# Element-wise steps of a fused linear-attention and GCU kernel offered to GpSimd, with a new fixed schedule

## The chip, the cores and the metric

The kernel runs on one core of a Trainium2 chip. The metric is the device time of one launch in microseconds (us), as the median over runs; lower is better.

## What is computed

Eight batches of eight heads, 576 tokens, head size 64, go through a linear attention, and the result through a two-matrix layer with a cosine gate:

```python
theta = np.pi / 2.0 * pos / S
def phi(x, c, s):                       # c, s: cos and sin of theta, one value per token
    r = np.maximum(x, 0.0)
    return np.concatenate([r * c, r * s], axis=-1)
q_p, k_p = phi(q, cos_w, sin_w), phi(k, cos_w, sin_w)
kv  = np.einsum('bhsf,bhsd->bhfd', k_p, v)
z   = np.sum(k_p, axis=2)
num = np.einsum('bhsf,bhfd->bhsd', q_p, kv)
den = np.einsum('bhsf,bhf->bhs', q_p, z)[..., None] + 1e-06
x   = (num / den)                       # then (4608, 512)
h   = x @ w_in                          # 512 -> 2048
g   = h * np.cos(h)
out = g @ w_out                         # 2048 -> 512
```

## The kernel before

**Stages.** The 4608 tokens are worked in nine chunks of 512. Chunks 0 to 7 hold 512 tokens of one batch each; the 64 tokens left over in each batch make chunk 8, the last one, which therefore has no attention of its own. For a batch, q, k and v are loaded in float32 (`load`), and for each of five token groups `t` and each of cosine and sine (`g`) one step `prep` makes a *feature*: a tile of 128 partitions by 512 elements, `max(x, 0)` times one value per partition, read as float32 and written as float16 into the tile `KQ`. That is 20 features a batch (10 of q, 10 of k; odd or even batches leave some of q out, so some have 18). `cast_v` copies v to float16. `kv` and `num` are the small attention matmuls, the result is normalised on VectorE (lines 449 to 453) and transposed. `layer1(c)` multiplies by `w_in` and applies the gate `h * cos(h)`: ScalarE takes the sine of `h + pi/2` into `ch` (line 503), then a multiplication makes `gT` (line 505). `layer2` multiplies by `w_out`.

**Seven products for eight.** `layer2` and a part of `layer1` do a 2 by 2 block product with seven block products and some additions (Strassen's way). In `layer1_fast` a group of four column blocks takes 28 matmuls of 256 columns in place of 16 of 512; its price is three copies on ScalarE (line 674) and three additions on VectorE (line 678) into the float32 SBUF tile `Z`. Two of its gates then read SBUF alone: one of 128x512 (from `Y`) and one of 128x1024 (line 695, from `U` and `Z` together). The rest of the gates read one operand from PSUM; no step of GpSimd in this kernel reads PSUM. `FAST1` says how many of the four groups of each chunk are done so.

**The order.** Nothing is scheduled while building. Every step is put on a list with `Plan.add`; `STARTS` holds a number for each step, and the steps are issued in the order of these numbers. `ENGS` holds a letter for each step: P TensorE, D VectorE, A ScalarE, G GpSimd, S the SP queue. A step made by `either` has code for several engines and the letter chooses. On each engine the instructions run in that order; between engines, semaphores hold the data dependences. Steps marked `port=True` (features, casts of v, sums and differences with both operands in SBUF, SBUF gates) get one thing more: where one of them on VectorE (D) follows one on GpSimd (G) in the list, or the other way round, a semaphore makes the later one wait for the earlier one (line 1091). So VectorE and GpSimd never work on such steps at the same time. I call a run of marked GpSimd steps between two marked VectorE steps a *turn*. VectorE steps that are not marked (gates from PSUM, additions from PSUM, normalisations) may run during a turn.

**GpSimd before.** It casts v in batches 2 to 7 (three steps a batch, line 360), issues the weight loads, and issues the stores of the output (lines 731, 744, 748) and two pairs of accumulating copies (line 818). It computes no feature and no gate. There are seven turns. The features of batches 2 to 7 stand on ScalarE (88) and VectorE (26), those of batches 0 and 1 on both as well (17 and 21).

Of the kernel before, what the change touches and what calls it, by code (L numbers as in the profile page):

```python
# [11 lines left out]
ALU = mybir.AluOpType  # L12
# [6 lines left out]
    53, 0, 0, 74, 139, 204, 269, 334, 399, 464, 543, 1050, 1190, 1280, 1100, 1370, 2014, 2134, 2044,  # L19
    843, 841, 923, 1134, 801, 717, 865, 1541, 885, 779, 969, 1524, 759, 717, 819, 1298, 1014, 1050,  # L20
    1174, 1245, 1112, 1287, 1092, 1203, 1050, 1380, 1236, 1422, 1430, 1329, 1393, 1354, 1473, 1504,
    1498, 1467, 1447, 1487, 1561, 1636, 1635, 1708, 1733, 1860, 1745, 1995, 2030, 1720, 1696, 1745,
    1831, 1921, 1956, 2018, 1983, 2080, 2030, 2208, 2270, 1896, 1909, 1965, 2098, 2133, 2121, 2220,
    2290, 2231, 2330, 2400, 2456, 2555, 2625, 2369, 2468, 2538, 2543, 2642, 2712, 2718, 2817, 2887,
    2630, 2730, 2800, 2805, 2904, 2974, 2979, 3078, 3148, 2892, 2991, 3061, 3066, 3166, 3384, 3241,
    3340, 3445, 3154, 3253, 3323, 3489, 3626, 3707, 3576, 3738, 3936, 3402, 3576, 3646, 1812, 1852,
    1917, 1792, 1982, 2047, 3802, 3922, 3832, 1772, 1752, 2284, 2349, 2662, 2893, 3590, 3514, 3506,
    3676, 4262, 3390, 3548, 3788, 3768, 3452, 3852, 3850, 4033, 4091, 3810, 4123, 4252, 4358, 3894,
    3962, 4297, 4355, 4039, 4296, 4512, 4639, 3997, 4024, 4467, 4524, 4160, 4086, 4211, 4185, 4186,
    4304, 4259, 4237, 4222, 4330, 4343, 4405, 4479, 4584, 4596, 4711, 4846, 4891, 4559, 4571, 4596,  # L30
    4806, 4841, 4834, 4869, 4933, 5301, 5611, 4781, 4794, 4818, 5054, 5089, 5189, 5164, 5630, 5756,
    5791, 3688, 3912, 3861, 4539, 4079, 4589, 4609, 5139, 4881, 5279, 5323, 5777, 7362, 7472, 5583,
    6356, 5953, 6207, 9668, 7417, 5213, 5313, 5569, 5077, 5189, 5340, 5866, 6065, 6146, 5779, 6015,
    6085, 5496, 5903, 6006, 6300, 6399, 6478, 6213, 6337, 6417, 6125, 6225, 6295, 6598, 6757, 6881,
    6511, 6645, 6715, 6710, 6869, 6942, 7007, 7155, 7230, 6797, 6981, 7064, 7107, 7206, 7423, 7416,
    7540, 7692, 7194, 7368, 7484, 5038, 5165, 8219, 9256, 4387, 4322, 4517, 4687, 4452, 4849, 5487,
    5425, 5443, 5401, 5549, 5527, 5363, 5485, 5735, 5661, 6134, 6024, 6244, 6449, 6387, 6585, 5838,
    5880, 5940, 5953, 5841, 6081, 6275, 5964, 6470, 5922, 6449, 6761, 6698, 6685, 6776, 6984, 7256,
    7094, 6972, 7125, 7393, 7428, 7281, 7293, 7318, 7528, 7640, 7503, 7515, 7587, 7725, 7760, 6552,
    7814, 7941, 6885, 7306, 7590, 7551, 7638, 7753, 8497, 8390, 8650, 9257, 8131, 8935, 9060, 9330,  # L40
    9418, 9836, 9616, 9789, 10202, 11508, 11870, 9963, 10050, 10149, 11705, 10219, 7872, 7994, 8097,
    7958, 8056, 8158, 8044, 8230, 8333, 8218, 8342, 8436, 8304, 8454, 8653, 8478, 8576, 8793, 8564,
    8662, 8732, 8762, 8898, 8968, 9047, 9145, 9370, 8849, 8948, 9029, 9244, 9431, 9536, 9505, 9603,
    9733, 9133, 9481, 9958, 9703, 9801, 10019, 9877, 9975, 10141, 10187, 10285, 10467, 5631, 5795,
    6886, 6966, 6269, 6334, 6807, 6523, 7478, 6919, 7306, 7031, 7093, 7545, 6695, 6666, 7082, 7192,
    7302, 7748, 7810, 7934, 7810, 7872, 7954, 8168, 8055, 8250, 8392, 8106, 8539, 8280, 8394, 8846,
    8712, 8836, 9240, 8750, 8737, 8854, 9050, 9034, 9022, 9090, 9383, 9219, 9232, 9431, 9554, 9604,
    9591, 9628, 9751, 10162, 10137, 10263, 10949, 7003, 9195, 9897, 10080, 10589, 10764, 11104,
    10273, 10448, 10757, 10919, 11248, 11498, 12495, 11378, 11478, 11857, 11776, 12496, 12595,
    11950, 12149, 12773, 12731, 12967, 13314, 13496, 14205, 13055, 13272, 13371, 13441, 14370,  # L50
    10368, 10401, 10434, 11071, 10360, 10416, 10404, 10528, 10607, 10703, 10597, 10657, 10640,
    10707, 10876, 11010, 10832, 10888, 11103, 11218, 11192, 11247, 11437, 10684, 10869, 10949,
    11007, 11359, 11559, 11578, 11757, 11954, 11093, 11645, 11893, 11335, 11595, 11664, 11725,
    12093, 12320, 11707, 11807, 11863, 11919, 11907, 12015, 12037, 12093, 12211, 12381, 12106,
    12161, 12259, 12323, 12421, 12609, 12409, 12533, 12712, 12645, 12881, 12951, 12237, 12831,
    13253, 7605, 7670, 8474, 8971, 8664, 7735, 9307, 8998, 8504, 8611, 9195, 9531, 9794, 9369, 8774,
    9653, 9388, 9498, 9608, 10535, 10770, 11043, 9851, 9715, 10079, 10466, 10025, 10664, 10335,
    9913, 10417, 10807, 10981, 11174, 11179, 11235, 11332, 11538, 11466, 11565, 11620, 11743, 11751,
    11763, 11788, 11911, 12081, 12093, 12154, 12277, 13139, 13375, 13789, 13471, 13602, 13707,
    13775, 13906, 14086, 15133, 14079, 14167, 14359, 14695, 14782, 14899, 14496, 15068, 15308,  # L60
    15377, 15892, 16236, 17499, 17279, 15464, 15551, 15713, 15783, 15838, 12876, 13106, 13073,
    13531, 12880, 12936, 12924, 13012, 13533, 13728, 13228, 13284, 13359, 13421, 13427, 13564,
    13558, 13625, 13757, 13903, 13862, 13955, 14025, 13142, 13843, 14147, 13689, 14067, 14313,
    14297, 14471, 14587, 13993, 14571, 14814, 14254, 14309, 14452, 14526, 14949, 15072, 14409,
    14521, 14608, 14663, 14651, 14753, 14894, 15011, 15173, 15369, 14938, 15061, 15247, 15291,
    15663, 15733, 14981, 15501, 15588, 15639, 15763, 15873, 15204, 15551, 15649, 9876, 9941, 11452,
    11336, 10854, 10789, 11533, 11409, 11695, 11471, 12297, 12031, 10919, 12359, 11969, 11297,
    11760, 11595, 11448, 12818, 12583, 13172, 12645, 12670, 12730, 13110, 13489, 13614, 12471,
    12769, 12875, 13048, 12707, 13970, 12986, 12834, 14196, 13402, 13415, 14208, 14331, 14396,
    14384, 14421, 15154, 14595, 14583, 14648, 14771, 14869, 14882, 14906, 15029, 15155, 15180,  # L70
    15483, 16450, 15947, 16122, 16592, 16153, 16284, 16383, 16569, 16700, 17266, 17943, 16787,
    16918, 17154, 17334, 17224, 17402, 17818, 18067, 17315, 17601, 17837, 18296, 18513, 18625,
    19136, 19316, 18122, 18209, 18401, 18471, 18526, 19226, 19046, 15794, 16297, 15840, 16391,
    15849, 15904, 15980, 16061, 16215, 16330, 16110, 16165, 16240, 16296, 16371, 16531, 16415,
    16470, 16631, 16767, 16657, 16717, 16881, 16483, 16581, 16706, 16023, 16953, 17047, 17005,
    17104, 17718, 17116, 17378, 17468, 16875, 17003, 17246, 17302, 17478, 17548, 17203, 17428,
    17545, 17601, 17502, 17779, 17775, 17840, 17919, 18057, 17992, 18117, 18213, 17905, 18239,
    18358, 17688, 18189, 18485, 18383, 18675, 18745, 18035, 18351, 18588, 12441, 12506, 13549,
    13739, 13096, 13014, 13583, 13686, 13645, 14117, 14837, 13471, 13893, 14005, 14999, 14409,
    14035, 14260, 14145, 15787, 15725, 15954, 15383, 15321, 15465, 14775, 14713, 14896, 15813,  # L80
    15601, 15960, 15111, 15259, 16741, 16458, 16471, 16942, 17398, 17092, 17104, 17150, 17273,
    17302, 17290, 17363, 17523, 17489, 17589, 17613, 17736, 18819, 18946, 19442, 19228, 19414,
    19513, 18811, 18942, 19041, 20535, 19687, 19774, 19873, 19943, 19998, 20439, 20915, 21027,
    20171, 20302, 20632, 21177, 21438, 21537, 21733, 21643, 21002, 21089, 21463, 21588, 21533,
    22885, 22975, 18419, 18452, 18649, 19060, 18469, 18575, 18600, 18682, 18761, 19198, 18768,
    18871, 18899, 18954, 19184, 19259, 19054, 19320, 19399, 19556, 19501, 19650, 19836, 19098,
    19277, 19381, 19327, 19700, 19775, 19973, 20071, 20291, 19600, 19923, 20125, 19544, 19600,
    19930, 20003, 20121, 20352, 19886, 19973, 20128, 20183, 20072, 20413, 20259, 20474, 20682,
    20788, 20526, 20582, 20710, 20570, 20768, 21007, 20742, 21077, 21190, 20829, 20927, 21129,
# [92 lines left out]
def kernel(  # L182
# [9 lines left out]
    nc = tc.nc  # L192
    B, H, S, D = q.shape
# [89 lines left out]
    pl = Plan()  # L283
# [839 lines left out]
```

## Time and profile before

| what | value |
|---|---|
| median of 3 runs | 282.94 us (282.44 to 284.58) |
| the profiled execution | 285.63 us, its span 283.9 us |
| granted clock of TensorE, mean | 0.984 |
| busy: TensorE matmul | 96% of the span |
| busy: VectorE, ScalarE, GpSimd | 85%, 72%, 20% |
| HBM read and written | 36.75 and 11.80 MB |

A profiled execution is one run; its span is the time from its first to its last instruction, and the run's own time is 1.7 us longer. The "busy" share of an engine counts only time in instructions. Matmuls overlap, so the duration of a single matmul is longer than the spacing from one to the next; what a matmul costs is read from the spacing.

### The profile page before, as it was taken

The numbers are of one execution on the slowest core, as the hardware profiler recorded it, in microseconds if no ns is written. First come the engines' busy times: TensorE is split into PE (matmuls) and PEld (weight loads), VectorE is DVE, ScalarE is ACT, GpSimd is POOL, SyncE is SP. The second block draws the span as 40 slices with busy tenths as digits, with TensorE's granted clock in tenths as the row PEclk, the third lists the DMA queues.
The fourth block names the chain that finished last, engine by engine and source line by source line (L and its number), as shares of the span: only waits on it lengthen the run. The fifth ranks groups of instructions, "written<-read, shape, count | busy, mean of one in ns | idle before, by whom it ended". The sixth has DMA issues, their size and how long they took to land.

```text
span 283.9 us, 6672 instructions
## 1 busy us (share of the span) xinstructions
PE 272.2 (96%) x2635; PEld 210.9 (74%) x2635; DVE 241.3 (85%) x447; ACT 205.3 (72%) x357; POOL 57.7 (20%) x87
## 2 busy tenths in 40 slices
PE   7699999999999999999999999999999999999993
PEld 2557857669976677877867777787768888876882
DVE  1666798999999999997989999999998979987742
ACT  2646699589989979998988959995736687676030
POOL 1322020021500310140150102415101343230410
PEclk9599999999999999999999999999999999999998
DMA  6999989969999999999998999989323949693515
GB/s 190 316 189 241 256 270 217 354 192 242 238 341 240 262 226 191 209 339 258 291 229 199 216 324 200 220 189 163 102 57 95 180 120 110 172 134 67 113 74 148
DMA packets 80222, 58.01 MB, mean 204 GB/s; under 512 B 43200, under 2 KB 77248, under 8 KB 80192
## 3 DMA queue, kind: packets, MB, share of 16 engines
q1 hardware_dynamic: 68960, 39.99, 59.0%
q0 software_dynamic: 10496, 17.04, 28.4%
q10 hardware_dynamic: 736, 0.57, 0.7%
q8 instruction: 20, 0.33, 0.5%
q14 instruction: 10, 0.08, 0.1%
HBM read 36.75 MB, written 11.80 MB: 171 GB/s over the span
## 4 chain that ended last, share of the span: by engine, by line
PE 77%; DMA 10%; DVE 5%; ACT 3%; issue 1%; POOL 1%; SPq 1%; ACTq 0%; DVEq 0%
PE M L860 28%; PE M L562 10%; PE M L530 9%; PE M L666 9%; PE M L785 5%; PE TR L666 4%; DMA qT<-KQ 3%; DMA vm<-in_v_dram 3%; PE ATT L433 3%; PE TR L562 2%; PE ATT L371 2%; DMA qm<-in_q_dram 2%; DMA out_dram<-ost 2%; PE M L400 2%; PE ATT L944 2%
## 5 line engine op out<-in xcount | busy, mean ns | idle before, releaser
L860 PEld LDWEIGHTS <-gT 128*128 128x128 f16 x560 | 54.4, 98 | 10.1 <-issue 0.8
L503 ACT ACTIVATE ch<-M 128x512 f32<-128x512 f32 x85 | 49.8, 596 | 11.4 <-PE M L530 5.0
L860 PE MATMUL M<-w_out_sb,gT 128*128 128x256 f16 x448 | 57.1, 273 | 0.5 <-ACT ost L871 0.5
L505 DVE TENSOR_TENSOR gT<-M,ch 128x512 f16<-128x512 f32 x78 | 52.1, 685 | 5.1 <-ACT ch L503 5.0
L871 ACT ACTIVATE ost<-M 128x512 f32<-128x512 f32 x41 | 24.3, 597 | 21.8 <-PE M L860 17.7
L344 ACT ACTIVATE KQ<-km,CS 128x512 f16<-128x512 f32 x56 | 38.5, 719 | 1.3 <-DMA km<-in_k_dram 1.3
L562 PE MATMUL M<-xT,w_in_sb 128*128 128x512 f16 x160 | 39.1, 379 | 0.0
L344 ACT ACTIVATE KQ<-qm,CS 128x512 f16<-128x512 f32 x49 | 33.8, 718 | 5.2 <-DMA qm<-in_q_dram 5.2
L562 PEld LDWEIGHTS <-w_in_sb 128*128 128x128 f16 x224 | 21.1, 98 | 17.7
L860 PE MATMUL M<-T,S 128*128 128x256 f16 x256 | 32.2, 273 | 0.0
L530 PE MATMUL M<-xT,w_in_sb 128*128 128x256 f16 x256 | 30.2, 273 | 0.8 <-DVE gT L505 0.8
L360 POOL CAST V<-vm 128x1024 f16<-128x1024 f32 (+1 forms) x18 | 15.9, 912 | 68.7 <-DMA vm<-in_v_dram 24.0
L860 PEld LDWEIGHTS <-S 128*128 128x128 f16 x256 | 24.8, 98 | 4.1
L530 PEld LDWEIGHTS <-w_in_sb 128*128 128x128 f16 x256 | 24.4, 98 | 4.4 <-issue 0.7
L666 PEld LDWEIGHTS <-w_in_sb 128*128 128x128 f16 x216 | 20.7, 98 | 3.4
L453 DVE TENSOR_TENSOR x<-ATT,rec 128x512 f16<-128x512 f32 x32 | 22.1, 692 | 1.3 <-DVE rec L451 0.2
L731 POOL DMA_DIRECT2D out_dram<-ost x20 | 10.8, 545 | 48.8 <-ACT ost L871 35.9
L678 DVE TENSOR_TENSOR Z<-M,Z 128x512 f32<-128x512 f32 x26 | 17.6, 686 | 2.4 <-PE M L666 1.2
L433 PEld LDWEIGHTS <-qT 128*128 128x128 f16 (+1 forms) x320 | 14.3, 101 | 5.1 <-issue 1.9
L674 ACT ACTIVATE Z<-M 128x512 f32<-128x512 f32 x22 | 12.9, 597 | 6.6 <-PE M L666 6.4
L748 POOL DMA_DIRECT2D out_dram<-ost x12 | 6.7, 566 | 52.9 <-ACT ost L871 52.9
L503 ACT ACTIVATE ch<-TR 128x512 f32<-128x512 f32 x17 | 10.2, 599 | 9.4 <-PE TR L666 5.0
(144 smaller groups left out, 473.8 us busy)
## 6 DMA issues: line engine op xcount, KB each, us to landing
out_dram<-ost POOLq DMA_DIRECT2D x38, 256.0 KB, 4.0
qm<-in_q_dram SPq DMA_DIRECT2D x8, 640.0 KB, 6.7
km<-in_k_dram SPq DMA_DIRECT2D x8, 640.0 KB, 7.0
qm<-in_q_dram SPq DMA_DIRECT2D x8, 512.0 KB, 5.7
km<-in_k_dram SPq DMA_DIRECT2D x8, 512.0 KB, 5.3
vm<-in_v_dram SPq DMA_DIRECT2D x6, 640.0 KB, 7.4
vm<-in_v_dram SPq DMA_DIRECT2D x6, 512.0 KB, 7.0
w_in_sb<-in_moe_w_in_dram POOLq DMA_DIRECT2D x4, 512.0 KB, 9.1
```

The lines of the kernel that those rows point to most:

```text
L344: fn = {"ACT": lambda: nc.scalar.activation(out=out_, in_=in_, func=AF.Relu, scale=sc), "DVE": lambda: nc.vector.tensor_scalar(out=out_, i ...
L360: "POOL": lambda: nc.gpsimd.tensor_copy(out=out_, in_=in_)}
L433: nc.tensor.matmul(bank[hb][ps, hh * D1:(hh + 1) * D1], lhsT=x[:, h, :], rhs=z[:, h, :], start=True, stop=True)
L453: nc.vector.tensor_tensor(out=split(x16[n][:, hs, :], k), in0=A[:, :, :, 0:D], in1=split(rec[n][:, hs], k).unsqueeze(3).broadcast_to((P, k ...
L503: act(0.5, due, lambda: nc.scalar.activation(out=ch[c], in_=bank, func=AF.Sin, bias=math.pi / 2.0, scale=1.0), [key], [("ch", c)])
L505: mul(due, 0.61, lambda q: q.tensor_tensor(out=dst, in0=bank if len(dst.shape) == 2 else bank.rearrange("p (j s) -> p j s", j=dst.shape[1] ...
L530: nc.tensor.matmul(M1[m][:, jj * 2 * P:(jj + 1) * 2 * P], lhsT=w_in_sb[:, cc, j * P:(j + 1) * P], rhs=X[:, cc, ts], start=(cc == 0), stop= ...
L562: nc.tensor.matmul(M, lhsT=w_in_sb[:, cc, j * P:(j + 1) * P], rhs=X[:, cc, :], start=(cc == 0), stop=(cc == NCT - 1))
L666: nc.tensor.matmul(bank[0][:, j * TH:(j + 1) * TH], lhsT=a(cc, j), rhs=b[:, cc, :], start=(first and j == 0 and cc == 0), stop=(last and j ...
L678: dve(0.61, due + 0.3, lambda: nc.vector.tensor_tensor(out=dst, in0=bank[0], in1=dst, op=ALU.add), [bank[1], key], [key])
L860: nc.tensor.matmul(bank[0][:, tt * MH:(tt + 1) * MH], lhsT=a[:, j, tt * P:(tt + 1) * P], rhs=b[:, j, :], start=(first and (apart or tt == ...
L871: act(0.5, due, lambda: nc.scalar.activation(out=dst, in_=view(bank), func=AF.Copy), [bank[1]], dk)
```

## The change

Three things. A feature of batches 2 to 7 may also be made on GpSimd, with the same two operations. The SBUF gates of `layer1_fast` may also be made there, for any chunk. The last chunk, 8, does all four groups of layer 1 with seven products (two before). Then both tables are new from the first entry to the last, so the whole order differs, and `ENGS` picks: 36 features go to GpSimd (14 leave VectorE, 22 leave ScalarE), 11 of the 16 gates of 128x512 and 5 of the 16 gates of 128x1024. The rule for turns is the old one; there are 24 turns in place of seven.

```diff
+    PREP_POOL = 0.65
@@ def prep
-        cost = {"DVE": 0.09 + 0.33 * f, "ACT": 0.12 + 0.5 * f}
+        cost = {"DVE": 0.09 + 0.33 * f, "ACT": 0.12 + 0.5 * f, "POOL": PREP_POOL}
         fn = {"ACT": lambda: nc.scalar.activation(out=out_, in_=in_, func=AF.Relu, scale=sc),
               "DVE": lambda: nc.vector.tensor_scalar(
+                  out=out_, in0=in_, scalar1=0.0, scalar2=sc, op0=ALU.max, op1=ALU.mult),
+              "POOL": lambda: nc.gpsimd.tensor_scalar(
                   out=out_, in0=in_, scalar1=0.0, scalar2=sc, op0=ALU.max, op1=ALU.mult)}
-        either(due, {e: c for e, c in cost.items() if eng in (e, "")}, fn, rd, wr)
+        either(due, {e: c for e, c in cost.items() if eng in (e, "") and (e != "POOL" or b > 1)},
+               fn, rd, wr)
@@ def mul
         if pool is None:
             dve(cost, due, lambda: fn(nc.vector), rd, wr)
-        elif pool:
-            pl.add("POOL", 0.15 + 1.9 * cost, 0.3 + 1.9 * cost, due, lambda: fn(nc.gpsimd), rd, wr,
-                   port=True)
         else:
-            dve(cost, due, lambda: fn(nc.vector), rd, wr, port=True)
+            either(due, {"DVE": cost, **({"POOL": 0.15 + 1.9 * cost} if pool else {})},
+                   {"DVE": lambda: fn(nc.vector), "POOL": lambda: fn(nc.gpsimd)}, rd, wr)
@@
-    FAST1 = {3:2,4:2,5:2,6:2,7:4,8:2}
+    FAST1 = {3:2,4:2,5:2,6:2,7:4,8:4}
-    Y_POOL, UZ_POOL = (), ()
+    Y_POOL, UZ_POOL = range(B + 1), range(B + 1)
```

The numbers beside the engines are inputs of the search that made the tables; they have no effect on the chip. In the built program one instruction is new that no source line asks for: ahead of the first feature on GpSimd stands a reload of that engine's code library. The old program has none. Also new in the order: the first two of the four loads of `w_out` are issued ahead of the loads of k and q of batch 1, behind them before.

## The prediction

> **What bounds the kernel now.** I read the busy times by stage first, then what ended the waits of VectorE and TensorE, then the chain of waits for the price of a matmul, then the groups of instructions by shape.
>
> ```profile
> core 0: us, PE busy (x) PEld busy (x) DVE busy (x) ACT busy (x) POOL busy (x), PEclk, DMA share, GB/s
> 0.00:20.00 20.00, 15.13 (x119) 8.89 (x120) 9.18 (x23) 9.42 (x16) 4.83 (x15) 0.83 0.90 233
> 20.00:36.00 16.00, 15.30 (x147) 12.22 (x144) 11.44 (x27) 9.51 (x17) 1.69 (x3) 1.00 1.17 249
> 36.00:52.00 16.00, 15.56 (x182) 10.91 (x182) 14.57 (x41) 14.30 (x26) 1.84 (x3) 1.00 0.97 251
> 52.00:68.00 16.00, 16.00 (x168) 11.77 (x167) 15.24 (x28) 12.53 (x23) 2.60 (x3) 1.00 0.93 250
> ...
> 140.00:160.00 20.00, 19.55 (x185) 14.93 (x183) 18.34 (x35) 17.43 (x30) 3.60 (x5) 1.00 0.95 211
> 160.00:180.00 20.00, 20.00 (x217) 16.27 (x216) 18.86 (x36) 15.77 (x29) 4.61 (x8) 1.00 1.08 271
> ```
>
> Each row is a stretch with the busy us of each engine. From 52 us on TensorE is busy in every microsecond but two half ones (19.50 of 20 from 120 to 140, 19.55 from 140 to 160), at full clock. So TensorE sets the time, and VectorE is close behind: from 52 to 180 us, the stage of the attention of batches 2 to 7, its seven rows sum to 120.6 of 128 us (15.24, 15.36, 15.02, 19.57, 18.20, 18.34, 18.86). GpSimd has room. An engine that frees VectorE therefore wins nothing by itself; one that holds VectorE up by more than some 7 us in this stage costs time.
>
> ```profile
> DVE gT L505 <- ACT ch L503: 6.4, 15, 1.4
> POOL V L360 <- DMA km<-in_k_dram: 20.8, 1, 20.8
> PE M L530 <- DVE gT L505: 0.8, 2, 0.5
> ```
>
> These are waits: who, for whom, total, times, longest. No row has VectorE waiting for GpSimd: the seven turns of before are free. TensorE, where it waits, waits for a gate on VectorE, which empties its PSUM bank.
>
> ```profile
> 83.52 0.87 PE M L860 x8
> 84.39 1.73 PE M L562 x8
> ```
>
> The chain of waits gives spacings: 8 matmuls of 256 columns in 0.87 us, 0.109 each, and 8 of 512 in 1.73, 0.216 each.
>
> ```profile
> L360 POOL CAST V<-vm 128x1024 f16<-128x1024 f32 x12 | 12.5, 1057 | 55.5 <-DMA km<-in_k_dram 20.8 <-DVE den L449 18.5 <-DMA vm<-in_v_dram 10.8
> L345 DVE TENSOR_SCALAR KQ<-km,CS 128x512 f16<-128x512 f32 x24 | 11.6, 512 | 1.2 <-DMA km<-in_k_dram 1.2
> L360 POOL CAST V<-vm 128x512 f16<-128x512 f32 x6 | 3.7, 620 | 13.2 <-DMA vm<-in_v_dram 13.2
> ```
>
> These are the only large computing steps of GpSimd: a cast of 512 elements takes 0.62 us, of 1024 1.06. It does no arithmetic in the trace and reads no value per partition.
>
> **The last chunk.** Two more groups by seven products: each drops 16 matmuls of 512 columns (16 x 0.216 = 3.46 us) and adds 28 of 256 (28 x 0.109 = 3.05). TensorE gains 2 x 0.41 = 0.8 us on the path. It adds 6 copies on ScalarE (0.60 each) and 6 additions on VectorE (0.69 each) between 240 and 272 us, where these engines are busy 17.1 and 26.7 of 32 us; they hide in the idle 15 and 5 us. Without that cover they would cost up to 4 us.
>
> **What leaves VectorE and ScalarE.** In the stage from 52 to 180 us VectorE loses 14 features (back to back 0.39 us each, 5.5 us), five 512-gates (0.60 each, 3.0) and two 1024-gates (1.14 each, 2.3): 10.8 us. Its room there grows from 7.4 to 18.2 us. ScalarE loses 22 features (0.72 each); it was not the bound. Neither moves the end.
>
> **What GpSimd gets.** The change makes waits: VectorE's next marked step stands behind the whole turn, and in order behind that step stand the gates that empty PSUM, for which TensorE waits; on GpSimd's own queue the output stores stand behind the features. So a turn is free only while its length stays under the unmarked VectorE work that the new order puts between the marked steps around it. The features' 13 turns, in order, as (features, other GpSimd work in us, VectorE's cover in us): (1, 0, 1.6), (1, 2.6, 4.2), (2, 3.1, 6.7), (3, 0, 1.8), (4, 0, 3.4), (3, 1.6, 4.0), (3, 4.9, 9.0), (4, 0, 3.0), (1, 2.2, 4.5), (5, 3.8, 5.7), (2, 1.2, 3.4), (1, 0, 0.6), (6, 4.9, 7.3). Other work is casts at 0.50 and 1.05 us (their spacing), stores at 0.54, a gate at 1.2, a large gate at 2.2. Cover is gates and additions at 0.60 and a normalisation at 1.04 (spacings). With p us for a feature, VectorE waits 36p + 24.3 - 55.2 = 36p - 31 where all turns are too long; at p = 0.62 two turns are short by 1.1 each, 2.3 in all.
>
> A gate's price: below, one read of the same length, the cast, 0.62 and 1.06; above, two reads, as twice the elements cast (1.06; and 1.06 + 1024 x 0.85 ns = 1.93) with a quarter more for the multiplication, 1.3 and 2.4. I take 1.2 and 2.2. The eleven turns with gates or casts alone wait 2 to 4 us by either end, nearly all after 200 us, where VectorE is idle 9 us from 200 to 272: nothing.
>
> **The price p.** Low end: the cast of the same shape and types, 0.62. High end: two passes (2 x 0.62), and each of the two operations started anew on each of the 8 rows of 64 elements like the smallest cast of the trace (2x4 elements, 0.19 us): 1.24 + 16 x 0.19 = 4.3. No row of GpSimd has arithmetic, two operations or a value per partition, and the new program has to load code for it; I find the cast near in shape only and take the middle, 2.45.
>
> By the Trainium skill (GPSIMD Engine Reference, 4.1 Engine selection) one-input element-wise work on GpSimd runs at roughly line rate, and the casts agree: 512 more elements cost 0.437 us, 0.85 ns each. By that rule p is the low end, and the sum is the first rival below. The same page (3.1) gives about 12 cycles an element where the code branches on data; at its 1.2 GHz that would be an estimate of 5.1 us a feature and some 417 us for the kernel.
>
> **Loads and code.** The reload of the code library has no row; GpSimd was idle 20.8 us ahead of its first cast (above), and the first feature now stands in that gap, so I take nothing; a load past some 10 us would delay batch 2 by the excess. Two `w_out` loads (1 MB each) move ahead of k and q of batch 1. The DMA share is 1.17 and 0.97 from 20 to 52 us, so the same bytes land at the same time in another order: nothing, between -1.1 us (TensorE's idle from 20 to 52 goes) and +2.
>
> **Sum.** At p = 2.45: waits 36 x 2.45 - 31 = 57.2; VectorE's room takes 18.2; 39.0 go to the path; less 0.8. That is +38.2 on a span of 283.9 (one run of 285.6; the median of the runs is 282.9, and I put the difference on that): 321.1 us.
>
> **Rivals.**
> First, features at the cast's price (p up to 1.2): waits of 2.3 to 16 us, under the room of 18.2, so VectorE holds nobody up, and only TensorE's 0.8 us remains: 282.1 us, not slower. For it: the rate of the casts, and no VectorE wait on GpSimd before. Against: one pass without arithmetic is not a feature. It decides below p = 1.3 (36p - 31 is short of the clipped sum there, 15.7 at 1.2 and 24.5 at 1.5; 1.5 gives 24.5 - 18.2 - 0.8, 288.4 us). Chance 0.30.
> Second, features dearer than my high end: each further microsecond adds 36; p = 4.3 gives 154.8 - 31 - 18.2 - 0.8 = 104.8, 388 us, and this case lies above it. For it: nothing in the trace bounds a software loop. Against: the casts' rate. Chance 0.11.
> Third, cheap features, and a better head: TensorE idles 4.9 us before 20 us and 1.1 to 52 us; half of that and the 0.8 would give 279.1 us. Against: the head waits for q's first load (VectorE idles 6.4 us for it), which stands where it stood. Chance 0.03.
> That the change does nothing of what it says is out: 36 features and 16 gates stand on GpSimd in the built order.
>
> **Numbers.** Forecast (p from 1.2 to 4.3): 0.56. The time is its middle, 321 us. The range takes in the first rival with 1 us below it and the forecast's upper end, 281 to 388 us, and leaves out 0.14. Signs differ between the cases; the forecast's own range is 283 to 388. Within 1% is 280.1 to 285.8, about what a measurement of this kernel can tell from no change: the first rival and the forecast's lowest prices (p under 1.4), 0.31. Faster by over 1%: the third, 0.03. Slower: 0.66.
>
> **What would show it.** A group of GpSimd features of 128x512 with its mean: under 1.2 us the forecast falls, and the first rival stands. Waits of VectorE's marked steps (XS, S, WS, gates from Z) for GpSimd: some 57 us in all, or next to none. TensorE's busy rows from 80 to 180 us: broken by waits for gates, or full as before. A wait of GpSimd's first feature behind the code load. For the last chunk: 56 more matmuls of 256 columns, 32 fewer of 512, and no new wait of TensorE after 240 us. If features are cheap and the kernel is still slower, the step that treats the gates, the stores or the head as free is wrong.

## The result and the profile after

The changed kernel takes 319.34 us (median of 4 runs, 317.64 to 320.94), the kernel before 283.27 us beside it (4 runs, 282.44 to 284.58): 1.127 times as long, 95% interval 1.119 to 1.135. The profiled execution is one of the four: 320.94 us, span 319.2. Its span is 35.3 us longer than that of before. Ratios and their intervals, here and below, leave out a run that took over 1.5% longer than the fastest of the same kernel.

The stages again, with the same columns as before the change (busy us of each engine, then TensorE's granted clock):

```profile
core 0: us, PE busy (x) PEld busy (x) DVE busy (x) ACT busy (x) POOL busy (x), PEclk, DMA share, GB/s
0.00:20.00 20.00, 15.99 (x151) 8.73 (x151) 12.13 (x34) 10.32 (x18) 6.26 (x14) 1.00 0.96 240
20.00:36.00 16.00, 15.92 (x144) 13.52 (x143) 11.05 (x21) 11.18 (x20) 0.53 (x4) 1.00 1.17 265
36.00:52.00 16.00, 15.04 (x184) 9.96 (x183) 14.88 (x40) 13.47 (x25) 1.73 (x3) 1.00 1.00 259
52.00:68.00 16.00, 16.00 (x167) 12.04 (x165) 13.88 (x25) 14.35 (x26) 6.57 (x5) 1.00 0.91 262
...
84.00:100.00 16.00, 10.68 (x78) 6.43 (x77) 7.63 (x14) 10.48 (x19) 11.53 (x6) 1.00 1.08 256
...
140.00:160.00 20.00, 14.89 (x114) 10.82 (x110) 12.79 (x21) 11.76 (x20) 9.75 (x6) 0.83 1.05 215
160.00:180.00 20.00, 16.41 (x160) 12.54 (x158) 10.91 (x24) 12.83 (x22) 19.79 (x15) 0.98 0.58 139
...
240.00:272.00 32.00, 32.00 (x291) 26.59 (x289) 26.05 (x46) 21.34 (x38) 15.26 (x15) 1.00 0.66 130
```

Up to 68 us TensorE is as busy as before, and from 240 to 272 us it is busy throughout. In between TensorE has holes, VectorE is less busy than before (12.79 of 20 us where it was 18.34), and GpSimd more. An engine that is less busy while the program gets slower is waiting. For what, the waits of VectorE say, and one row of TensorE (who, for whom, total, times, longest):

```profile
DVE gT L697 <- POOL gT L507: 9.9, 2, 8.5
DVE gT L507 <- ACT ch L505: 8.9, 24, 0.9
DVE XS L625 <- POOL KQ L349: 7.7, 2, 5.1
...
PE ATT L376 <- POOL V L365: 7.2, 3, 5.3
...
DVE gT L899 <- POOL KQ L349: 6.2, 1, 6.2
...
DVE T L810 <- POOL KQ L349: 3.6, 1, 3.6
```

None of the rows with POOL was there before. All such rows of VectorE in the changed kernel add up to 42.8 us. The marked steps wait for the last step of a GpSimd turn, a feature (`KQ`, L349) or what stands behind the features in the same turn. The groups of GpSimd by shape:

```profile
L349 POOL TENSOR_SCALAR KQ<-km,CS 128x512 f16<-128x512 f32 x18 | 35.7, 1992 | 16.3 <-PE ATT L438 12.6 <-PE M L564 3.6
L349 POOL TENSOR_SCALAR KQ<-qm,CS 128x512 f16<-128x512 f32 x18 | 35.7, 1989 | 11.5 <-DVE WS L604 7.4 <-DVE gT L899 2.5 <-ACT ch L505 1.5
...
L697 POOL TENSOR_TENSOR gT<-Z,ch 128x1024 f16<-128x1024 f32 x4 | 9.6, 2394 | 9.2 <-ACT ch L691 7.8 <-DVE gT L899 1.4
L507 POOL TENSOR_TENSOR gT<-Z,ch 128x512 f16<-128x512 f32 x6 | 7.6, 1266 | 16.2 <-DVE S L838 9.5 <-ACT ch L505 6.3 <-DVE den L454 0.4
L365 POOL CAST V<-vm 128x512 f16<-128x512 f32 x6 | 3.7, 611 | 0.0
```

So p, the price of a feature on GpSimd, is 1.99 us: over three times the cast of the same shape (0.61), four times the feature on VectorE (0.51 before). The prediction took 2.45. One turn in the timeline, on the three engines (start, length, what ran, the idle time ahead of it and what ended that):

```profile
start us, us, engine line op out<-in xcount [idle before <-releaser]
91.25 7.91 POOL L349 TENSOR_SCALAR KQ<-km,CS 128x512 f16<-128x512 f32 x4 [3.63 <-PE M L564]
...
99.20 0.69 DVE L604 TENSOR_TENSOR w_in_sb<-w_in_sb 128x1024 f16<-128x1024 f16 x1 [4.66 <-POOL KQ L349]
...
100.94 0.68 DVE L507 TENSOR_TENSOR gT<-M,ch 128x512 f16<-128x512 f32 x1
...
101.68 1.87 PE L564 MATMUL M<-xT,w_in_sb 128*128 128x512 f16 x4 [4.14 <-DVE gT L507]
```

Four features take 7.91 us. VectorE's next marked step waits 4.66 us for them; behind it in VectorE's order stands a gate that empties a PSUM bank, and TensorE waits 4.14 us for that gate. Three other long turns look alike: VectorE waits 3.63 us and TensorE 2.87 at 87 us, 5.06 and 4.28 at 146 us, 6.20 and 5.33 at 176 us. In these four nearly the whole wait of VectorE comes out at TensorE; only 0.5 to 0.9 us is lost on the way. That is not what the sum of the prediction did with it. Two turns differ. At 117 us VectorE waits 2.66 us and TensorE 1.05. And while VectorE waits its longest, 8.54 us up to 219.5 us, what TensorE waits for, 5.27 us, is a cast of v (the row `PE ATT L376`) that stands behind the features in GpSimd's own order. In the whole run TensorE's waits grew from 7.0 to 32.5 us. The last four matmuls above also run at half speed (1.87 us for four); more on that below.

### The profile page after: what moved, and what is told of

Read it like the earlier page. It is cut to its first block, busy times and chain, and to the rows that moved or that the text cites. A ratio compares the mean times of both kernels' runs of the same rounds, so it can differ in the third digit from the quotient of the medians.

```text
span 319.2 us, 6778 instructions
## 1 busy us (share of the span) xinstructions
PE 281.6 (88%) x2659; PEld 215.6 (68%) x2659; DVE 228.7 (72%) x421; ACT 196.0 (61%) x339; POOL 155.5 (49%) x139
## 4 chain that ended last, share of the span: by engine, by line
PE 39%; POOL 17%; issue 6%; DVE 5%; ACT 1%; POOLq 0%; DVEq 0%; ACTq 0%
PE M L862 20%; POOL KQ L349 11%; PE M L668 9%; PE TR L668 3%; PE M L564 3%; POOL V L365 3%; PE TR L564 2%; PE ATT L376 1%; POOL gT L507 1%; DVE Z L680 1%; POOL out_dram L733 1%; PE ATT L438 1%; DVE gT L899 1%; DVE S L838 1%; DVE XS L625 1%
## 5 line engine op out<-in xcount | busy, mean ns | idle before, releaser
L505 ACT ACTIVATE ch<-M 128x512 f32<-128x512 f32 x80 | 47.0, 596 | 52.9 <-PE M L564 24.1
L862 PE MATMUL M<-w_out_sb,gT 128*128 128x256 f16 x448 | 56.4, 273 | 0.4 <-DVE gT L899 0.4
L564 PE MATMUL M<-xT,w_in_sb 128*128 128x512 f16 x160 | 42.0, 398 | 4.1 <-DVE gT L507 4.1
L349 POOL TENSOR_SCALAR KQ<-km,CS 128x512 f16<-128x512 f32 x18 | 35.7, 1992 | 16.3 <-PE ATT L438 12.6
L349 POOL TENSOR_SCALAR KQ<-qm,CS 128x512 f16<-128x512 f32 x18 | 35.7, 1989 | 11.5 <-DVE WS L604 7.4
L862 PE MATMUL M<-T,S 128*128 128x256 f16 x256 | 33.2, 277 | 2.9 <-DVE T L810 2.9
L346 ACT ACTIVATE KQ<-km,CS 128x512 f16<-128x512 f32 x44 | 30.4, 719 | 1.7 <-DMA km<-in_k_dram 1.7
L346 ACT ACTIVATE KQ<-qm,CS 128x512 f16<-128x512 f32 x39 | 26.6, 717 | 4.3 <-DMA qm<-in_q_dram 4.3
L376 PEld LDWEIGHTS <-KQ 128*128 128x128 f16 x320 | 12.6, 104 | 9.9 <-issue 7.7
L668 PEld LDWEIGHTS <-WS 128*128 128x128 f16 x144 | 13.7, 99 | 8.3 <-DVE XS L625 4.9
```

Of the source, the lines that this page charges most:

```text
L346: fn = {"ACT": lambda: nc.scalar.activation(out=out_, in_=in_, func=AF.Relu, scale=sc), "DVE": lambda: nc.vector.tensor_scalar(out=out_, i ...
L349: "POOL": lambda: nc.gpsimd.tensor_scalar(out=out_, in0=in_, scalar1=0.0, scalar2=sc, op0=ALU.max, op1=ALU.mult)}
L505: act(0.5, due, lambda: nc.scalar.activation(out=ch[c], in_=bank, func=AF.Sin, bias=math.pi / 2.0, scale=1.0), [key], [("ch", c)])
L564: nc.tensor.matmul(M, lhsT=w_in_sb[:, cc, j * P:(j + 1) * P], rhs=X[:, cc, :], start=(cc == 0), stop=(cc == NCT - 1))
L668: nc.tensor.matmul(bank[0][:, j * TH:(j + 1) * TH], lhsT=a(cc, j), rhs=b[:, cc, :], start=(first and j == 0 and cc == 0), stop=(last and j ...
L862: nc.tensor.matmul(bank[0][:, tt * MH:(tt + 1) * MH], lhsT=a[:, j, tt * P:(tt + 1) * P], rhs=b[:, j, :], start=(first and (apart or tt == ...
```

## Experiments

Theory L, formed on this trace: what a turn is longer than its cover goes to the end one to one; VectorE's idle time in other places of the stage takes nothing of it. Its rivals: T, the 24 turns and the new order cost the time whatever a feature costs; G, the gates or the rest of the new table; R, the prediction's own, in which VectorE's room of the stage takes the first 18 us; Q, GpSimd's own queue is late; H, the two engines hold each other up in memory, turns or not; and the halved clock as a second cost of its own. (In the expectations written before the rivals were sorted, the price through the turns is called theory P.) All kernels are timed beside the kernel before on the same chip, whose median was 282.97 to 283.88 us.

**The price alone.** Same order, turns and operands; another pair of operations. The maximum is left out, so this kernel does not compute the full result.

```diff
-  nc.gpsimd.tensor_scalar(out=out_, in0=in_, scalar1=0.0, scalar2=sc, op0=ALU.max, op1=ALU.mult)
+  nc.gpsimd.tensor_scalar(out=out_, in0=in_, scalar1=4.0, scalar2=sc, op0=ALU.add, op1=ALU.mult)
```

> The 36 features on GpSimd are computed with the operations add 4.0 and multiply in place of max 0 and multiply: the maximum is left out, all else (order, turns, operands, number of instructions) is that of the changed kernel. Theory P (the price of a GpSimd feature, through the turns): if this pair of operations is cheaper than 1.99 us, at p the waits of VectorE shrink as 36p - 31; at some 0.7 us the mean of the group falls there, VectorE's waits on GpSimd fall from some 43 us to under 10, the four half-clock stretches are gone and the time is 281 to 285 us. Rival T (24 turns and the new order cost the time, whatever a feature costs): the time stays above 312 us though the group's mean falls. If the mean stays at 1.99 us the run tells nothing between them.

Measured: 282.16 us (10 runs), ratio 0.994 (0.991 to 0.998). The groups:

```profile
L349 POOL TENSOR_SCALAR KQ<-qm,CS 128x512 f16<-128x512 f32 x18 | 12.4, 689 | 15.7 <-DVE WS L604 5.3 <-DVE gT L899 5.1 <-ACT KQ L346 3.6
L349 POOL TENSOR_SCALAR KQ<-km,CS 128x512 f16<-128x512 f32 x18 | 12.4, 689 | 17.7 <-PE ATT L438 12.6 <-PE M L564 3.6
```

One operation in place of another takes the feature from 1.99 to 0.69 us and the kernel from 319 to 282. Its turns are the 24 of the changed kernel, so T falls. VectorE still waits 8.3 us for GpSimd, 6.3 of them in turns that have a gate and no feature; these cost nothing that shows.

**Features back.** The 36 features go to ScalarE and VectorE; the gates on GpSimd and the new order stay. First 22 and 14, spread evenly; then each feature where the kernel before had it.

```diff
-ENGS: 36 features "G"
+ENGS: 22 of them "A", 14 "D"                  (first)
+ENGS: every feature the letter of before      (second)
```

> The 36 GpSimd features go to ScalarE (22) and VectorE (14); gates, casts, stores and the new order stay. Theory P: with no feature on GpSimd the long stalls and half-clock stretches go, 282 to 286 us. Rival G (the gates on GpSimd, or the rest of the new table): over 300 us.

> All features of q and k on the engines that the kernel before gave them (those 36 of GpSimd: 32 on ScalarE and 4 on VectorE; of the others 18 from ScalarE to VectorE, 8 the other way); gates, casts, stores and the rest of the new order stay. If the 1.8% that the changed kernel without GpSimd features lost to the kernel before came from how the 36 were shared out there, the time is 281 to 285 us; if it comes from the new order or the gates on GpSimd, it stays at 287 to 291 us.

Measured: 288.95 us (ratio 1.018, 1.012 to 1.024) and 290.29 us (1.027, 1.024 to 1.030). The long stalls and the half-clock stretches after 20 us are gone, as expected. But both are 5 to 7 us slower than the kernel before, more than expected. The second run rules out that my sharing out of the features did it. So the new order, with its gates on GpSimd but without cheap features there, is worse than the old one; its small waits of TensorE lie from 80 to 140 and from 170 to 190 us (ends of waits: VectorE's and ScalarE's steps). What in the order makes them was not isolated.

**Gates back.** The 16 gates go back to VectorE, the features stay.

```diff
-ENGS: 11 gates of 128x512 and 5 of 128x1024 "G"
+ENGS: the same "D"
```

> The 16 gates of operands in SBUF go back from GpSimd to VectorE; the 36 features stay. Theory P: 36 features at 1.99 us still make 40 us of turn waits; ScalarE no longer waits for GpSimd's gates (11 us in its waits) and VectorE's waits shrink a little: 306 to 318 us. Rival G (the gates): under 295 us.

Measured: 323.67 us, ratio 1.140 (1.133 to 1.147), outside the expected 306 to 318. ScalarE's waits for GpSimd went, as expected, but VectorE still waits 35.0 us for it, now for features and casts alone, and has the gates to do as well. G falls: the gates on GpSimd cost nothing, at best they save a little (the intervals overlap).

**No turns.** The semaphores between the two engines' marked steps are left out; waits for data stay.

```diff
-                if last is not None and last[0] != s["on"]:
-                    tc.add_manual_dep(ins.ins, last[1].ins.name, SYNC, reason="shared port")
```

> The semaphores that fix the turns of VectorE and GpSimd are left out; the order on each engine, and every wait for data, stays. Theory P says that the price counts because VectorE's marked steps stand behind the turn: without the turns some 40 us of waits lose their ground, and if nothing else holds VectorE while GpSimd works the time is under 295 us, with only waits for the data of the features left. Rival H (the two engines hold each other up at their memory port anyway): the waits turn into longer VectorE or GpSimd instructions in the same stretches and the time stays within 10 us of 319.

Measured: 306.33 us, ratio 1.080 (1.072 to 1.087): 13 us less than with turns, and 22 more than before. Neither expectation holds. VectorE's waits for GpSimd fall from 42.8 to 2.1 us. In their place, in the trace without turns:

```profile
ACT ch L505 <- POOL gT L507: 14.2, 2, 10.7
PE ATT L376 <- POOL V L365: 9.2, 2, 8.7
```

Now GpSimd's own queue is late: ScalarE waits for gates and TensorE for casts of v that stand behind features, up to 10.7 and 8.7 us at once. So VectorE lost 40.7 us of waits, and the time only 13. And the features got dearer, 2.22 us in the mean. In the timeline, the turn ahead of the wait of 8.7 us:

```profile
start us, us, engine line op out<-in xcount [idle before <-releaser]
190.07 1.68 DVE L697 TENSOR_TENSOR gT<-Z,ch 128x1024 f16<-128x1024 f32 x1 [0.21 <-ACT ch L691]
190.76 3.90 POOL L349 TENSOR_SCALAR KQ<-km,CS 128x512 f16<-128x512 f32 x1
191.68 1.21 DVE L899 TENSOR_TENSOR gT<-gT,S 128x2048 f16<-128x2048 f16 x1
194.66 1.98 POOL L349 TENSOR_SCALAR KQ<-qm,CS 128x512 f16<-128x512 f32 x1
```

A feature beside which two of VectorE's marked steps ran took 3.90 us, 1.92 more than the next one, which had no VectorE work beside it; those two steps overlap it for 2.20 us. So the turns are not the whole price: without them the two engines still hold each other up.

**Is it the order of the two operations?** Multiply first, then max, the full computation.

```diff
+  nc.gpsimd.tensor_scalar(out=out_, in0=in_, scalar1=sc, scalar2=0.0, op0=ALU.mult, op1=ALU.max)
```

> The GpSimd feature with its two operations in the other order: multiply by the scale, then max 0 (the scales are cosines and sines from 0 to pi/2, so the result is the same). Everything else as in the changed kernel. If the price hangs on which operation stands first, the mean falls to some 0.69 us and the time to 281 to 285 us with the full computation. If it hangs on the pair as such (no pair with the max of a multiply is cheap), the mean stays near 1.99 us and the time at 316 to 323 us. Rival T (turns, not price) is out after the run with add and multiply, so it is not tested again here.

Measured: 318.42 us, ratio 1.125 (1.122 to 1.127), 1.99 us a feature. The pair of max and multiply is dear in either order.

**A middle price.** Two cheap pairs in place of the dear one, the full computation.

```diff
+  one = nc.gpsimd.tensor_scalar(out=out_, in0=in_, scalar1=60000.0, scalar2=0.0, op0=ALU.min, op1=ALU.max)
+  two = nc.gpsimd.tensor_scalar(out=out_, in0=out_, scalar1=sc, scalar2=1.0, op0=ALU.mult, op1=ALU.mult)
```

> Each GpSimd feature as two instructions: min 60000 and max 0 into the f16 tile, then multiply by the scale and by 1.0 in place. The full computation, 36 more instructions on GpSimd. Theory P: two passes at about the 0.69 us of the run with add and multiply make p near 1.4, by 36p - 31 some 19 us of turn waits, just at VectorE's room of 18.2: 282 to 290 us, no half-clock stretch after 20 us. If each pass costs as much as the max-multiply pair (1.99), p is near 4 and the time 360 to 400 us. If waits begin to hurt well below 18 us, because a long turn stalls TensorE even while VectorE has room on average, the time is above 292 us.

Measured: 299.77 us, ratio 1.060 (1.056 to 1.064). The group rows (most line numbers are 6 higher here than in the changed kernel, and the feature has two lines):

```profile
L339 POOL TENSOR_SCALAR KQ<-KQ,CS 128x512 f16<-128x512 f16 x36 | 25.0, 696 | 3.4
...
L337 POOL TENSOR_SCALAR KQ<-qm 128x512 f16<-128x512 f32 x18 | 11.0, 612 | 12.9 <-DVE WS L610 6.3 <-DVE gT L905 3.0 <-ACT KQ L353 2.4
L337 POOL TENSOR_SCALAR KQ<-km 128x512 f16<-128x512 f32 x18 | 11.0, 612 | 17.4 <-PE M L538 12.6 <-DVE gT L905 3.5
```

p is 0.612 + 0.696 = 1.31 us, just the point below which the prediction had the kernel not slower, and it is 17 us slower than before: of the three things expected, the third. TensorE's clock was halved in three places after 20 us, where none was expected. VectorE waits 26.8 us for GpSimd here. Take off the 6.0 to 6.3 us of the turns without a feature, which every run of these has and which cost nothing in the cheap one, and the features' overruns are 2.0 us at 0.69, 20.5 at 1.31 and 36.8 at 1.99; the times are 282.2, 299.8 and 319.3. From the first to the last, 34.8 us more of waits for 37.1 us more of time. That fits theory L; R, by which the first 18 us are free, does not fit.

**Between 0.69 and 1.31.** The k features with the two instructions, the q features with add and multiply.

```diff
+  if not both:   # q
+      return nc.gpsimd.tensor_scalar(out=out_, in0=in_, scalar1=4.0, scalar2=sc, op0=ALU.add, op1=ALU.mult)
```

> Between the two cheap runs: the 18 GpSimd features of k as two instructions (min and max, multiply and multiply; 1.31 us in all), the 18 of q with add 4.0 and multiply (0.69 us; the max is left out in these). By the turns of the prediction, each turn's overrun cut off below at nothing, the features' waits of VectorE are 3.7 us at 0.69, 19.0 at 1.31 and here 9.0, or 5.3 more than in the run with add and multiply. Theory L (a turn's overrun goes to the end one to one, because VectorE's idle time elsewhere can't be used in advance): 282.2 + 5.3, so 286 to 289 us. Rival R (VectorE's room of the whole stage takes the first 18 us, as the prediction had it, and the run with two instructions is slow for another reason, such as more instructions): 281 to 284 us.

Measured: 289.07 and 292.35 us in the two fastest of four runs, 293.59 and 295.59 in the others; they give no interval. All four lie above R's band (281 to 284), and above L's upper end of 289 too, the first of them barely. VectorE's waits for GpSimd are 14.5 us, 8.2 without the turns that have no feature, where 9.0 was expected. So waits cost from under 10 us on already; the run doesn't tell whether one to one.

**Does the halved clock cost?** Dummy matmuls in two of the four long stalls.

```diff
+  for _ in range(count):   # 60 at 146 us, 75 at 213 us
+      nc.tensor.matmul(ATT[:, 0, 260:388], lhsT=IDENT, rhs=IDENT, start=True, stop=True)
```

> The changed kernel with dummy matmuls on TensorE ahead of two of its four long stalls, at 146 us (60 of 128 columns) and 213 us (75), into columns of the ATT bank that nothing reads; they add some 7.6 us of TensorE work inside the stalls and nothing else. Clock theory: the clock is halved after a 3.41 us interval of the profile in which TensorE did too little (share under some 0.42); with the fillers the half-clock stretches at 148.5 and 216.7 us are gone, those at 100.7 and 179.2 us stay, and the time falls by some 4 to 5 us (2.3 and 2.7 us of matmuls at half speed) to 314 to 316 us. If the half clock is only a mark in the records, or comes from something else than TensorE's idle time, the stretches stay or the time does not fall, 318 us or more.

First what it is about. Intervals of 3.41 us of the changed kernel, laid where its clock changes; in each, us, TensorE's busy us, and the clock in the third column from the end:

```profile
core 0: us, PE busy (x) PEld busy (x) DVE busy (x) ACT busy (x) POOL busy (x), PEclk, DMA share, GB/s
145.05:148.46 3.41, 1.41 (x13) 1.02 (x11) 0.00 (x0) 1.09 (x2) 3.41 (x3) 1.00 0.77 201
148.46:151.87 3.41, 1.13 (x5) 0.73 (x6) 2.54 (x6) 0.06 (x1) 0.83 (x1) 0.50 1.20 293
199.66:203.07 3.41, 1.46 (x8) 0.78 (x8) 1.54 (x4) 3.41 (x7) 3.34 (x4) 1.00 0.52 201
203.07:206.49 3.42, 3.31 (x36) 2.99 (x36) 3.10 (x9) 2.77 (x6) 3.42 (x3) 1.00 0.60 156
```

TensorE busy for 1.41 us of an interval (0.41 of it), and the next one has half the clock; busy for 1.46 (0.43), and it has the whole clock. With the dummies, in the first of the two places:

```profile
146.84:150.25 3.41, 2.84 (x51) 2.72 (x49) 1.13 (x3) 0.00 (x0) 2.25 (x2) 1.00 1.17 322
150.25:153.66 3.41, 3.12 (x25) 2.42 (x25) 3.38 (x7) 1.79 (x4) 0.00 (x0) 1.00 0.93 172
```

The clock stayed whole, there and after 213 us, as expected: TensorE's idle time makes the half clock. But the time hardly moved: 318.46 us, ratio 1.124 (1.119 to 1.128), against 1.127 (1.119 to 1.135) without dummies; 4 to 5 us had been expected. TensorE, 2.4 us ahead after the first place, waited longer in the next long stall (6.23 us in place of 5.33), as VectorE and GpSimd had not become faster. In the changed kernel the four half-clock stretches cost TensorE some 10 us (half of the 19.9 us that it is busy in them), but taking two of them away won under 1 us in the medians: TensorE then only waits longer for the next turn.

**Without turns, at the middle price.** Then also with the gates back on VectorE.

```diff
 (the two instructions of the middle price, and)
-                    tc.add_manual_dep(first.ins, last[1].ins.name, SYNC, reason="shared port")
```

> The two-instruction features (1.31 us together, the full computation), and the semaphores of the turns left out; order on each engine as before. Theory L: the 26.7 us that VectorE waited for GpSimd in the run with turns are what cost it 17 us; without turns they are gone, GpSimd has some 60 us less features than its room, and the time is 281 to 287 us. Rival Q (GpSimd's own queue: casts and gates come late behind the features whatever VectorE does): VectorE's waits go, TensorE's and ScalarE's waits for GpSimd's casts and gates grow, and the time stays above 293 us.

> As the run before this one, and the 16 gates of operands in SBUF back on VectorE. If what is left there is ScalarE's and VectorE's wait for GpSimd's gates, this is faster, 279 to 284 us, and at best a little under the kernel before; if VectorE lacks the 16 us of time that GpSimd took over, it is slower by 1 to 5 us.

Measured: 297.97 us (ratio 1.051, 1.047 to 1.055) and 294.15 us (three runs, 293.18 to 294.71; a fourth took 298.40; 1.036, 1.034 to 1.039). Q it is in the first: VectorE's waits for GpSimd go from 26.8 to 2.4 us, and only 2 of the 17 us come back; now ScalarE waits 11.3 us for GpSimd's gates and TensorE 4.4 for a cast of v, and the second instruction of a feature takes 0.91 us in place of 0.70. The second run takes ScalarE's wait away and gains 3.8 us, less than was expected; TensorE's wait for the cast of v (5.0 us at 187 us) is still there, because six features of the last batch stand around it in GpSimd's order. The expectation of 279 to 284 us failed.

**Only what the cover takes.** The middle price with turns, and in each turn only as many features as the prediction's list has cover for; 17 stay, 19 go to ScalarE.

```diff
-ENGS: 36 features "G"
+ENGS: the first 1, 1, 2, 1, 2, 1, 3, 2, 1, 1, 1, 0, 1 of the 13 turns "G", the others "A"
```

> The run with two-instruction features (1.31 us together, the full computation, turns fixed), but in each turn only as many of them as the unmarked VectorE work of that turn covers, by the list of the prediction: 1, 1, 2, 1, 2, 1, 3, 2, 1, 1, 1, 0 and 1, so 17 of 36; the other 19 go to ScalarE. Theory L: with no overrun VectorE waits for GpSimd some 8 us as with add and multiply (turns with gates), the long stalls are gone and the time is 283 to 288 us (up to the 7 us that all 36 features cost when they were put back). If features on GpSimd cost time in themselves, about in proportion to their number, half of the run's 17 us over the kernel before stays: 290 to 293 us.

Measured: 288.91 us, ratio 1.018 (1.011 to 1.026), 0.9 us above L's band and below the rival's 290 to 293; the interval, 286 to 291 us, does not part the two. The trace shows what is gone: VectorE's waits for GpSimd are 6.5 us, and of these only 0.2 us is for a feature. 17 features cost no wait of VectorE when their turns have cover. What is left over the kernel before is of the size of the runs with all features put back, and lies in part at the same place (173 to 183 us, where TensorE waits for ScalarE and VectorE).

No run with the full computation beats the kernel before. The run with add and multiply, 0.6% faster (0.2 to 0.9%), shows about what this order could win if a feature on GpSimd cost 0.69 us.

## Why the prediction was right, and where it was not

The time came within 1.7 us (321 against 319.34), and in the direction and by the mechanism forecast: VectorE's marked steps wait for turns that are too long, and TensorE for the gates behind them. But it is right in its sum by luck, only because two of its terms are wrong by about as much in opposite directions.

- **What bounds it:** right. TensorE was full, and an engine that holds VectorE up comes out at TensorE.
- **The waits, 36p - 31:** right. At the measured price it gives 36 x 1.99 - 31 = 40.6 us; the features' overruns in the trace are 36.8 (42.8 less 6.0 in turns without a feature). Turn by turn, cut off at nothing, the same list gives 3.7, 9.0, 19.0 and 41.1 us at the four prices run; measured 2.0, 8.2, 20.5 and 36.8. (At 0.62 it gives 2.6 us, not the 2.3 of the prediction; nothing hangs on that.)
- **The price p = 2.45:** too high. It is 1.99, which takes 36 x 0.46 = 16.6 us off the sum. The bounds (0.62 and 4.3) held it, but 2.45 was only their middle. Why this pair of operations is dear no run shows; the restarts on each row, which gave the high end, were not tested.
- **"VectorE's room takes 18.2; 39.0 go to the path":** this step failed. With the true price it would have given 40.6 - 18.2 - 0.8 = 21.6 us, a time some 15 us short. The runs at 0.69, 1.31 and 1.99 us show that the room takes next to nothing: 34.8 us of waits, 37.1 us of time. The room is real as a sum over the stage, but it lies in crumbs (VectorE's waits for ScalarE before the change: 6.4 us in 15 pieces, the longest 1.4) and can't be used ahead of time: a turn that runs 4.7 us over stops VectorE for 4.7 us in one place, and TensorE, which runs on for 0.5 to 0.9 us (from PSUM banks that are still free, as I read it), stands for the rest. The 18.2 us and the 16.6 us nearly cancel.
- **The point at p = 1.3 below which nothing is lost:** wrong with it. At 1.31 us 17 us are lost, and with half of the features at that price over 5.
- **The first rival,** features at the cast's price: its 282.1 us is what came out at 0.69 us (282.16), so the place of the cost is confirmed from the other end. It did not occur because the pair max and multiply is not at that price.
- **Gates at nothing:** right in the time. They cost 1.27 and 2.39 us, near the upper bounds; their turns make 6.3 us of waits of VectorE, more than the 2 to 4 us of the prediction, and these cost nothing in the run at 0.69 us. Putting the gates back gained nothing.
- **Code reload and moved `w_out` loads at nothing:** right in the time. The 12.6 us that GpSimd idles ahead of its first feature ended, by the profile, with TensorE's attention; a reload that fits into them does not show. TensorE is busy 30.96 us from 20 to 52 us, where it was 30.86.
- **The last chunk:** 56 more matmuls of 256 columns and 32 fewer of 512, as said, and TensorE has no wait from 219 us to the end, so the copies and additions hide. The 0.8 us itself was not measured alone.
- **Left out of the sum:** GpSimd's own queue. The prediction named the stores behind the features; what comes late are casts of v and gates. It took the place of the turns when they were taken away, and kept those kernels 11 to 22 us above the kernel before. In the changed kernel it is mostly inside the same stalls, as in the one that ends at 219 us; how much it would cost there by itself is not shown.

With these numbers the change closes: 36.8 us of overruns at one to one, less 0.8, are 36.0 us, where the medians lie 36.1 us apart and the spans 35.3. But one to one is a fit along one row of runs, and not the only one. The run with 17 features has no overrun and still takes 288.91 us; from it to the run with all 36 at the same price it is 20.3 us more of waits and only 10.9 us more of time. The 19 features that ScalarE does not have to make may be worth the difference (putting all 36 back cost 5 to 7 us over the kernel before), or a part of the waits is absorbed after all. The runs show that the 18.2 us are not free; what share of a wait comes out in general stays open. Of the head, the profiled run of before had an interval at half clock (0.83 from 0 to 20 us) that the one of after had not; that is a matter of the single execution, since other executions of the kernel before show a mean clock up to 1.000, and no part of the change.

## What to carry to other kernels

Here a wait was absorbed where it fell or hardly at all: hold the length of each single stop against the work that is buffered at that place (here PSUM banks for under 1 us of TensorE), not the sum of the stops against the idle time of a whole stage. Before work is moved to a slower engine that takes turns with another, count each turn by itself, its work against its cover, and look at what else stands behind that work in its own queue. And measure the price of the very instruction: the same shape with another pair of operations can cost a third.

## What the runs showed of the hardware

GpSimd's price of a tensor_scalar over 128x512 hangs on the pair of operations: add and multiply 0.69 us, min and max 0.61, multiply and multiply 0.70 (this one from float16, the others from float32), but max and multiply 1.99, in either order; a cast is 0.61. The Trainium skill (GPSIMD Engine Reference, 4.1 Engine selection) has one-input work at roughly line rate: three of the four pairs agree, the one that the kernel needs does not.

GpSimd and VectorE can hold each other up when both read SBUF: without turns, a feature took 3.90 us beside two of VectorE's two-operand steps, 1.98 without. The Trainium skill (SBUF — State Buffer, SBUF: two separate sides) says that a pair of ports is locked by the one for a whole instruction while the other waits; the sum above, 1.92 us more for 2.20 us beside it, agrees with that. In that run only features with a marked step of VectorE beside them took over 2.05 us, up to 4.02; beside unmarked steps alone they took 1.98 to 2.01. But not every overlap shows it: a feature at 83 us took 1.98 us with all 1.22 us of a marked two-operand step beside it, and at 156 us it was VectorE's step that became longer, 1.62 us in place of 1.21.

TensorE's clock in these records changes on a grid of 3.41 us. In the fourteen traces here an interval in which TensorE was busy for up to 0.42 of it was followed by one at half clock, and from 0.43 on by one at full clock; an interval at half clock had to be busy for 0.86 or more to be followed by a whole one (at 0.74 and 0.76 it was not). The Trainium skill (TensorE: Matmul & The Clock Gate, Part 1) has a free-running window of 3413 ns and the half clock after an idle window; the grid agrees, and the window need not be idle, only under some 0.42 busy.
